# Loading v of the first eight heads in long rows and turning it twice on chip

## The chip, the cores and the metric

The kernel runs on one core of a Trainium2 chip. The metric is device time in microseconds, the median of several runs. A profile of one execution, with every instruction and DMA packet of the core, stands beside it.

## The reference

Two stages follow each other. The first is causal attention for 4 batches, 8 heads, 768 positions and 64 elements per head. Some heads ("retrieval") see all earlier positions, the others only 4 sink positions and a window of 64. The second is a soft mixture of experts over the 3072 resulting rows of 512: 32 slots, 8 experts with 4 slots each, a softmax over the rows to fill the slots and one over the slots to bring the results back.

```python
scores = scale * np.matmul(q, k.transpose(0, 1, 3, 2))
...                                            # causal, sink and window masks per head
a = np.exp(scores - max); a = a / sum          # softmax
x = np.matmul(a, v)                            # -> rows (3072, 512)

logits = x @ phi                               # (3072, 32)
d = softmax(logits, axis=0)
slot_input = (d.T @ x).reshape(8, 4, 512)
for e in range(8):
    slot_out[e] = np.maximum(slot_input[e] @ w1[e], 0) @ w2[e]   # 512 -> 1024 -> 512
out = softmax(logits, axis=1) @ slot_out       # (3072, 512)
```

All inputs lie in HBM in fp32. The kernel loads them with a cast to bf16.

## The kernel before

Attention runs in 16 rounds, one for each pair of heads `n`. Loads are issued from GpSimd into one queue. q and k come in rows of 12 positions, 12 x 64 x 4 = 3072 bytes of HBM, and land with (head, 12 positions) on each partition; TensorE turns them to (64 elements of a head) x (768 positions) by 24 small transposes. v comes with position on the partition, as the product with the probabilities needs it, and so in pieces of 64 elements: 256 bytes in HBM, 128 in SBUF.

```python
def load_qk(pairs, order="qk"):
    t = raw.tile([P, 2, 2, S], BF16, tag="raw", name="raw")       # raw has two buffers
    ...
        nc.gpsimd.dma_start(t[:, z, :len(pairs)],
                            src[b, h:h + c].rearrange("(y h) (p s) d -> (h p) y (s d)", h=2, s=12))

def load_v(m):                                                    # four heads: pairs 2m, 2m + 1
    b, h = m // 2, 4 * (m % 2)
    nc.gpsimd.dma_start(vbs[m % 3].rearrange("p h j d -> p (h j) d")[:, :, :D],
                        v[b, h:h + 4].rearrange("h (j p) d -> p (h j) d", p=P))

def transposes(n, which):
    src = (qraw if which == "q" else kraw)[n]
    tp = trp.tile([P, 12, 64], BF16, tag="tr", name="tp" + which)  # PSUM, trp has two buffers
    for s in range(12):
        for hh in range(2):
            po = slice(64 * hh, 64 * hh + 64)
            nc.tensor.transpose(tp[po, s, :], src[po, 64 * s:64 * s + 64], ident[po, po])
    return tp

def evac(n, which, tp):                                           # PSUM -> SBUF
    dst = qkT.tile([P, S], BF16, tag="T" + which, name="T" + which)
    o, i = dst.rearrange("c (p s) -> c p s", s=12), tp.rearrange("c s p -> c p s")
    if which == "q":
        nc.vector.tensor_copy(o, i)
        qT[n] = dst
    else:
        nc.scalar.copy(o, i)
        kT[n] = dst

def vfar(n):                                                      # v, zeroed for far keys of window heads
    t = vfp.tile([P, 2, 4, 66], BF16, tag="vf", name="vf")
    nc.vector.tensor_mul(t, vb(n)[:, :, :4, :], fmask[:, h:h + 2])
```

A round computes the scores of pair n in six chunks on TensorE, each followed by an exp on ScalarE, and between them the product of the previous pair's probabilities with v (`pvmm`), its division (`norm`), the transposes of the next pair's q and k, and masks on VectorE. The schedule is by hand: each engine works in the order of the program.

```python
load_qk([0], "kq"); load_qk([1]); load_v(0); nc.gpsimd.dma_start(w1s[0], w1v[0])
...
for n in range(NP):                         # 16 pairs
    if n == 0:
        load_qk([2]); load_v(1)
    elif n == 1:
        load_qk([3])
    elif n == 2 or (n % 2 == 1 and n < 12):
        m = 2 if n == 2 else (n + 3) // 2
        load_qk([2 * m, 2 * m + 1]); load_v(m)
    w_load(1 + 5 * (n + 1) // 8)            # next w1, w2: 2 MB of HBM each
    scores(n, 0)
    ...                                     # pvmm(last, 0..2), logits
    scores(n, 1)
    ...                                     # norm(last, 0); transposes and evac of q of pair n + 1; mask(n, 0)
    scores(n, 2)
    ...                                     # pvmm(last, 3); x_transpose(n - 2); mask(n, 1)
    scores(n, 3)
    if 0 < n < NP - 1:
        tk = transposes(n + 1, "k")
    mask(n, 2)
    scores(n, 4)
    if 0 < n < NP - 1:
        evac(n + 1, "k", tk)
    if n >= 1:
        pvmm(last, 4)
    if n:
        vfar(n)
    scores(n, 5)
    if n == 0:
        vfar(0)
    if n >= 1:
        pvmm(last, 5)
        norm(last, 1)
    ...
    if n == 0:                              # pair 1 is turned at the end of round 0
        evac(1, "q", transposes(1, "q")); evac(1, "k", transposes(1, "k"))
    if n < 3:
        far_mask(n + 1)                     # VectorE: masks of the next two heads
        for h in (2 * n + 2, 2 * n + 3):
            head_mask(h)
    elif n == 3:
        setup_late()                        # VectorE: small tiles for the second stage
```

The second stage then fills the slots, multiplies by w1 and w2 and writes the output. The last three w2 go into the buffers of masks and probabilities and can only be loaded when attention is through, in halves of 256 columns: all left halves first, then all right ones. The left half of the first 12 output rows per partition is computed and written before the right halves of w2 are used; `second(e, (1,))` (line 513), `slot_out` (line 560) and the products (line 541) come after them.

Of the kernel before, what the change touches and what calls it, by code (L numbers as in the profile page):

```python
# [11 lines left out]
BF16 = mybir.dt.bfloat16  # L12
# [26 lines left out]
def kernel(  # L39
# [13 lines left out]
    nc = tc.nc  # L53
    P = 128
    B, H, S, D = q.shape
# [14 lines left out]
    xp = ent(tc.tile_pool(name="xp", bufs=2))  # L70
    scp = ent(tc.tile_pool(name="scp", bufs=2, space=PSUM))
    trp = ent(tc.tile_pool(name="trp", bufs=2, space=PSUM))
    pvp = ent(tc.tile_pool(name="pvp", bufs=2, space=PSUM))

    def single(shape, dt, name, tag=None):
        return singles.tile(shape, dt, name=name, tag=tag or name)
# [3 lines left out]
    ident = single([P, P], BF16, "ident")  # L80
# [23 lines left out]
    qraw, kraw, qT, kT, vf, pT, pv, xb = {}, {}, {}, {}, {}, {}, {}, {}  # L104

    def load_qk(pairs, order="qk"):
        b, h, c = pairs[0] // 4, 2 * (pairs[0] % 4), 2 * len(pairs)
        t = raw.tile([P, 2, 2, S], BF16, tag="raw", name="raw")
        for which in order:
            src, d, z = (q, qraw, 0) if which == "q" else (k, kraw, 1)  # L110
            nc.gpsimd.dma_start(t[:, z, :len(pairs)],  # L111
                                src[b, h:h + c].rearrange("(y h) (p s) d -> (h p) y (s d)", h=2, s=12))
            for x, n in enumerate(pairs):
                d[n] = t[:, z, x]

    def load_v(m):
        b, h = m // 2, 4 * (m % 2)
        nc.gpsimd.dma_start(vbs[m % 3].rearrange("p h j d -> p (h j) d")[:, :, :D],  # L118
                            v[b, h:h + 4].rearrange("h (j p) d -> p (h j) d", p=P))

    def vb(n):
        return vbs[n // 2 % 3][:, 2 * (n % 2):2 * (n % 2) + 2]
# [5 lines left out]
    def w_load(upto):  # L128
        while wi[0] < min(upto, 2 * NE - 3):
            e = wi[0] % NE  # L130
            dst, src = ((w1s, w1v), (w2s, w2v))[wi[0] // NE]
            nc.gpsimd.dma_start(dst[e], src[e])
            wi[0] += 1

    def transposes(n, which):
        src = (qraw if which == "q" else kraw)[n]
        tp = trp.tile([P, 12, 64], BF16, tag="tr", name="tp" + which)
        for s in range(12):
            for hh in range(2):
# [4 lines that stand above are left out]
    def evac(n, which, tp):  # L144
# [4 lines that stand above are left out]
            qT[n] = dst  # L149
        else:  # L150
            nc.scalar.copy(o, i)  # L151
            kT[n] = dst

    def vfar(n):
        h = 2 * (n % 4)
        t = vfp.tile([P, 2, 4, 66], BF16, tag="vf", name="vf")
        nc.vector.tensor_mul(t, vb(n)[:, :, :4, :], fmask[:, h:h + 2])
        vf[n] = t

    def scores(n, c):  # L160
        o, ln, parts = CHUNKS[c]
        sc = scp.tile([P, 2, 512], F32, tag="sc", name="sc")
        at = 0
        for j, i0, cnt in parts:
            for hh in range(2):
                po = 64 * hh
                nc.tensor.matmul(sc[:, hh, at:at + 128 * cnt], kT[n][po:po + 64, j * 128:(j + 1) * 128],  # L167
                                 qT[n][po:po + 64, i0 * 128:(i0 + cnt) * 128], start=True, stop=True)
            at += 128 * cnt
        if c == 0:  # L170
            pT[n] = ptp.tile([P, 2, NPT], BF16, tag="pT", name="pT")
        nc.scalar.activation(pT[n][:, :, o:o + ln], sc[:, :, :ln], ACT.Exp, scale=scale)  # L172

    def mask(n, c):
        h = 2 * (n % 4)
        if c == 0:
            x, m = pT[n][:, :, 0:512], msk[:, h:h + 2, 0:512]
        elif c == 1:
            x = pT[n][:, :, 512:1024].rearrange("p h (a c) -> p h a c", a=2)
            m0 = msk[:, h:h + 2, 256:512]  # L180
            m = bass.AP(tensor=m0.tensor, offset=m0.offset, ap=[m0.ap[0], m0.ap[1], [0, 2], [1, 256]])
        else:
            x, m = pT[n][:, :, 1024:1408], msk[:, h:h + 2, 256:640]
        nc.vector.tensor_mul(x, x, m)  # L184

    def pvmm(n, i):
        if i % 3 == 0:
            pv[n] = pvp.tile([P, 3, 2, 65], F32, tag="pv", name="pv")
        for hh in range(2):
            for j in range(i + 1):  # L190
                vv = vb(n) if i - j <= 1 else vf[n]
                o = BLK[j, i]
                nc.tensor.matmul(pv[n][:, i % 3, hh, :], pT[n][:, hh, o:o + 128], vv[:, hh, j, :D + 1],  # L193
                                 start=(j == 0), stop=(j == i))

    def norm(n, half):
        b, h = n // 4, 2 * (n % 4)
        if h == 0 and half == 0:
            xb[b] = xp.tile([P, 6, DM], BF16, tag="xb", name="xb")
        rs = small.tile([P, 3, 2, 1], F32, tag="rs", name="rs")  # L200
        nc.vector.reciprocal(rs, pv[n][:, :, :, 64:65])  # L201
        nc.vector.tensor_mul(  # L202
            xb[b][:, 3 * half:3 * half + 3, h * D:(h + 2) * D].rearrange("p i (h d) -> p i h d", h=2),
            pv[n][:, :, :, :64], rs.to_broadcast([P, 3, 2, 64]))
# [10 lines left out]
    def logits_mm(b, dbs):  # L215
        if b not in lgs:
            lgs[b] = trp.tile([P, 256], F32, tag="tr", name="lg")
        for db in dbs:
            for g in range(3):
                nc.tensor.matmul(lgs[b][32 * g:32 * g + 32, :], phi[:, db], xT[:, db, 256 * g:256 * (g + 1)],  # L220
                                 start=(db == 0), stop=(db == 3))

    def logits_exp(b):
        nc.scalar.activation(expT[:, b], lgs[b][:96], ACT.Exp, accum_out=colpart[:, b:b + 1])  # L224
# [16 lines left out]
    def slot_sum(b):  # L241
        sp = sps[b][0]
        if b == 0:
            nc.vector.tensor_copy(slot_acc, sp)
        else:
            nc.vector.tensor_add(slot_acc, slot_acc, sp)
# [44 lines left out]
    def head_mask(h):  # L291
        V.tensor_scalar(msk[:, h], grade, thr[:, h:h + 1], None, op0=ALU.is_ge)
# [27 lines left out]
    for n in range(NP):  # L320
        if n == 0:
            load_qk([2])
            load_v(1)
# [4 lines that stand above are left out]
            load_qk([2 * m, 2 * m + 1])  # L328
            load_v(m)
        w_load(1 + 5 * (n + 1) // 8)  # L330
        if n == 0:
            nc.gpsimd.dma_start(phi, moe_phi.rearrange("(do di) s -> di do s", di=P))
        b, r = n // 4 - 1, n % 4
        last = n - 1

        scores(n, 0)
        if n >= 1:
            for i in range(3):
                pvmm(last, i)
        if b >= 0 and r == 2:  # L340
            logits_mm(b, (0, 1, 2, 3))

        scores(n, 1)
        if b >= 0 and r == 2:
            logits_exp(b)
        if n >= 1:
            norm(last, 0)
        if 0 < n < NP - 1:
            tq = transposes(n + 1, "q")
            evac(n + 1, "q", tq)  # L350
        mask(n, 0)
        if b >= 0 and r == 3:
            exp_tokens(b)

        scores(n, 2)
        if n >= 1:
            pvmm(last, 3)
        if n >= 2:
            x_transpose(n - 2)
        mask(n, 1)  # L360
# [8 lines that stand above are left out]
            evac(n + 1, "k", tk)  # L369
        if n >= 1:  # L370
            pvmm(last, 4)
        if n:
            vfar(n)

        scores(n, 5)
        if n == 0:
            vfar(0)
        if n >= 1:
            pvmm(last, 5)
            norm(last, 1)  # L380
        if b >= 0 and r == 3:
            dispatch_mm(b)
            slot_sum(b)
        if n == 0:
            evac(1, "q", transposes(1, "q"))
            evac(1, "k", transposes(1, "k"))
        if n < 3:
            far_mask(n + 1)
# [3 lines that stand above are left out]
            setup_late()  # L392
# [212 lines left out]
```

The softmax here doesn't subtract the row's maximum and nothing guards it: scores larger than these inputs give would overflow.

## Time and profile before

| what | value |
|---|---|
| time, median of 3 runs (lowest to highest) | 157.29 us (156.19 to 157.38) |
| span of the profiled execution | 155.7 us |
| busy: TensorE, VectorE, ScalarE | 118.2 (76%), 106.8 (69%), 109.8 (71%) us |
| DMA packets (of these under 512 bytes) | 40535 (26050) |
| v loads: number, size in SBUF, median time from issue to landing | 8, 384 KB, 13.0 us |
| q, k loads of the same size: median time to landing | 6 each, 10.2 and 11.4 us |
| DMA issue on GpSimd: a v load, a q or k load (mean) | 1451 ns, 639 ns |

In the 40 equal slices of the span each digit is the busy share in tenths (9 is 90% or more); PEclk is the granted clock of TensorE, DMA the share of the 16 DMA engines.

```profile
DVE  2896269999987869978769979678735414429700
ACT  3286489979799998999898999999451512408700
PEclk9975559999999999999999999999999999956975
DMA  3999999999999999999999999999999999977995
```

The groups of section 5 give for each line of the kernel, engine and operation the count, the busy time, the mean duration of one, and the idle time before it with what ended it. The three copies that matter for the change are these:

```profile
L148 DVE COPY Tq<-tpq 128x768 bf16<-128x768 bf16 x16 | 15.3, 956 | 4.8 <-PE tpq L141 4.6
L151 ACT COPY Tk<-tpk 128x768 bf16<-128x768 bf16 x16 | 12.9, 805 | 5.0 <-PE tpk L141 5.0
L211 DVE COPY xT<-tpx 128x768 bf16<-128x768 bf16 (+1 forms) x17 | 9.0, 528 | 0.8 <-PE tpx L210 0.8
```

L is the line in the kernel, DVE is VectorE, ACT ScalarE, PE TensorE (PEld its weight loads), POOL GpSimd.

### The profile page before, as it was taken

The page shows a single profiled execution, that of the slowest core. Times are in us where ns is not written, and L with a number is a line of the kernel's source. Part 1 is how long each engine was busy: PE and PEld are TensorE (multiplying, and loading weights), DVE is VectorE, ACT ScalarE, POOL GpSimd, SP SyncE. Part 2 cuts the span into 40 slices and gives each one's busy share as a digit, 9 for nine tenths or more (in the row PEclk, how much of TensorE's full clock was granted, in tenths as well). Part 3 has the DMA queues.
Part 4 walks back from the last instruction along what each step waited for, and adds up shares of the span by engine and source line. Part 5 has one row for each costly group of instructions (what it writes and reads, how often), then busy time and mean ns, then how long its engine had stood idle before and what let it go on. Part 6 is the DMA issues. An engine that isn't in the chain of part 4 may idle for free. (4 is left out here: it accounts for less than half of the span.)

```text
span 155.7 us, 5051 instructions
## 1 busy us (share of the span) xinstructions
PE 118.2 (76%) x2239; PEld 74.6 (48%) x2239; DVE 106.8 (69%) x247; ACT 109.8 (71%) x148; POOL 41.1 (26%) x57
## 2 busy tenths in 40 slices
PE   6756598878697979977979979778987897449500
PEld 2324365555465645755656556555633476214300
DVE  2896269999987869978769979678735414429700
ACT  3286489979799998999898999999451512408700
POOL 7673043720350260170084200000480000700000
PEclk9975559999999999999999999999999999956975
DMA  3999999999999999999999999999999999977995
GB/s 54 155 184 203 172 218 203 196 187 189 212 219 202 188 216 198 186 222 195 186 219 200 185 211 223 213 217 215 210 223 190 199 196 199 240 290 283 404 355 183
DMA packets 40535, 32.85 MB, mean 211 GB/s; under 512 B 26050, under 2 KB 37826, under 8 KB 38594
## 3 DMA queue, kind: packets, MB, share of 16 engines
q0 software_dynamic: 38208, 27.82, 115.1%
q1 hardware_dynamic: 2306, 4.72, 8.1%
q8 instruction: 17, 0.28, 0.7%
q14 instruction: 4, 0.03, 0.1%
HBM read 52.49 MB, written 6.29 MB: 377 GB/s over the span
## 5 line engine op out<-in xcount | busy, mean ns | idle before, releaser
L172 ACT ACTIVATE pT<-sc 128x1024 bf16<-128x1024 f32 (+1 forms) x96 | 83.4, 923 | 9.3 <-PE sc L167 8.8
L167 PE MATMUL sc<-Tq,Tk 64*128 64x256 bf16 (+3 forms) x320 | 36.5, 292 | 13.6 <-ACT Tk L151 10.0
L193 PEld LDWEIGHTS <-pT 128*128 128x128 bf16 x672 | 24.9, 99 | 12.2 <-issue 8.0
L184 DVE TENSOR_TENSOR pT<-pT,msk 128x1024 bf16<-128x1024 bf16 (+1 forms) x48 | 29.3, 639 | 0.2 <-ACT pT L172 0.2
L193 PE MATMUL pv<-vb,pT 128*128 128x65 bf16 x352 | 27.5, 196 | 0.3 <-DVE xb L202 0.3
L193 PE MATMUL pv<-vf,pT 128*128 128x65 bf16 x320 | 25.3, 197 | 0.0
L167 PEld LDWEIGHTS <-Tk 64*128 64x128 bf16 x320 | 11.2, 95 | 22.6 <-ACT Tk L151 13.2
L141 PEld LDWEIGHTS <-raw 64*64 64x64 bf16 x768 | 15.9, 115 | 10.8 <-issue 7.4
L111 POOL DMA_DIRECT2D raw<-in_q_dram x10 | 6.4, 639 | 49.5 <-PE tpk L141 48.3
L148 DVE COPY Tq<-tpq 128x768 bf16<-128x768 bf16 x16 | 15.3, 956 | 4.8 <-PE tpq L141 4.6
L202 DVE TENSOR_TENSOR xb<-pv,rs 128x384 bf16<-128x384 f32 x32 | 17.8, 557 | 1.1
L151 ACT COPY Tk<-tpk 128x768 bf16<-128x768 bf16 x16 | 12.9, 805 | 5.0 <-PE tpk L141 5.0
L201 DVE RECIPROCAL rs<-pv 128x6 f32<-128x6 f32 x32 | 6.2, 193 | 11.9 <-PE pv L193 11.9
L118 POOL DMA_DIRECT2D vb<-in_v_dram x8 | 11.6, 1451 | 1.1 <-issue 0.9
L141 PE MATMUL tpk<-ident,raw 64*64 64x64 bf16 x384 | 9.8, 202 | 2.3 <-DVE Tq L148 1.3
L399 POOL DMA_DIRECT2D w<-in_moe_w_dram x6 | 5.2, 879 | 22.3 <-PE sc L167 20.1
L141 PE MATMUL tpq<-ident,raw 64*64 64x64 bf16 x384 | 9.6, 200 | 1.7 <-DMA raw<-in_q_dram 1.7
L541 PE MATMUL bank<-slot_out,expR 128*128 128x256 bf16 (+1 forms) x36 | 9.2, 368 | 1.9 <-DVE slot_out L556 0.5
L210 PE MATMUL tpx<-ident,xb 128*128 128x128 bf16 x96 | 8.1, 218 | 2.0 <-ACT expT L224 1.1
L211 DVE COPY xT<-tpx 128x768 bf16<-128x768 bf16 (+1 forms) x17 | 9.0, 528 | 0.8 <-PE tpx L210 0.8
L543 ACT ACTIVATE ot<-bank,rrow 128x512 f32<-128x512 f32 x6 | 3.9, 686 | 6.5 <-PE bank L541 6.5
L541 PEld LDWEIGHTS <-expR 128*128 128x128 bf16 x36 | 5.1, 153 | 6.3 <-issue 5.7
(86 smaller groups left out, 117.3 us busy)
## 6 DMA issues: line engine op xcount, KB each, us to landing
w<-in_moe_w_dram POOLq DMA_DIRECT2D x13, 1024.0 KB, 18.3
vb<-in_v_dram POOLq DMA_DIRECT2D x8, 384.0 KB, 13.0
w<-in_moe_w_dram POOLq DMA_DIRECT2D x6, 512.0 KB, 17.8
raw<-in_q_dram POOLq DMA_DIRECT2D x6, 384.0 KB, 10.2
raw<-in_k_dram POOLq DMA_DIRECT2D x6, 384.0 KB, 11.4
out_dram<-ot SPq DMA_DIRECT2D x2, 1024.0 KB, 4.6
out_dram<-oh SPq DMA_DIRECT2D x3, 512.0 KB, 6.3
out_dram<-oh POOLq DMA_DIRECT2D x2, 512.0 KB, 6.8
```

The lines of the kernel that those rows point to most:

```text
L118: nc.gpsimd.dma_start(vbs[m % 3].rearrange("p h j d -> p (h j) d")[:, :, :D], v[b, h:h + 4].rearrange("h (j p) d -> p (h j) d", p=P))
L141: nc.tensor.transpose(tp[po, s, :], src[po, 64 * s:64 * s + 64], ident[po, po])
L148: nc.vector.tensor_copy(o, i)
L151: nc.scalar.copy(o, i)
L167: nc.tensor.matmul(sc[:, hh, at:at + 128 * cnt], kT[n][po:po + 64, j * 128:(j + 1) * 128], qT[n][po:po + 64, i0 * 128:(i0 + cnt) * 128], s ...
L172: nc.scalar.activation(pT[n][:, :, o:o + ln], sc[:, :, :ln], ACT.Exp, scale=scale)
L184: nc.vector.tensor_mul(x, x, m)
L193: nc.tensor.matmul(pv[n][:, i % 3, hh, :], pT[n][:, hh, o:o + 128], vv[:, hh, j, :D + 1], start=(j == 0), stop=(j == i))
L202: nc.vector.tensor_mul(xb[b][:, 3 * half:3 * half + 3, h * D:(h + 2) * D].rearrange("p i (h d) -> p i h d", h=2), pv[n][:, :, :, :64], rs. ...
L210: nc.tensor.transpose(tp[:, i * 128:(i + 1) * 128], xb[b][:, i, hp * 128:(hp + 1) * 128], ident)
L211: nc.vector.tensor_copy(xT[:, hp, i0 * 128:i1 * 128], tp[:, i0 * 128:i1 * 128])
L541: nc.tensor.matmul(op, er[r], slot_out[:, cs], start=True, stop=True)
```

## The change

The first two v loads (the eight heads of batch 0, pairs 0 to 3) take the same form as q and k: rows of 3072 bytes of HBM, landing in a tile of their own. Its buffer is one of the two that later hold the attention output `xb`. What lands is not yet what the product needs, so v is turned twice: 24 small transposes and a ScalarE copy bring it to (head, element) x position, in the same way as k; then six transposes of 128 x 128 and a VectorE copy bring position onto the partitions, into the same `vbs` tile as before. This happens in the rounds 0 to 3, each for its own pair, just before `vfar`. The other six v loads stay as they are. It is meant to spare the queue the small packets at the start, when the rounds wait for data.

```diff
+    vraw = xp.tile([P, 2, 2, S], BF16, tag="xb", name="vraw")
+
     def load_v(m):
         b, h = m // 2, 4 * (m % 2)
+        if m < 2:
+            nc.gpsimd.dma_start(vraw[:, m], v[b, h:h + 4].rearrange("(y h) (p s) d -> (h p) y (s d)", h=2, s=12))
+            return
         nc.gpsimd.dma_start(vbs[m % 3].rearrange("p h j d -> p (h j) d")[:, :, :D],
                             v[b, h:h + 4].rearrange("h (j p) d -> p (h j) d", p=P))
@@
     def transposes(n, which):
-        src = (qraw if which == "q" else kraw)[n]
+        src = vraw[:, n // 2, n % 2] if which == "v" else (qraw if which == "q" else kraw)[n]
@@
             nc.scalar.copy(o, i)
-            kT[n] = dst
+            if which == "k":
+                kT[n] = dst
+            return dst
+
+    def v_blocks(n):
+        vT = evac(n, "v", transposes(n, "v"))
+        tp = trp.tile([P, 6, P], BF16, tag="tr", name="tpv")
+        for j in range(6):
+            nc.tensor.transpose(tp[:, j, :], vT[:, 128 * j:128 * j + 128], ident)
+        nc.vector.tensor_copy(vb(n).rearrange("p h j d -> p j h d")[:, :, :, :D], tp.rearrange("p j (h d) -> p j h d", h=2))
@@
         if n >= 1:
             pvmm(last, 4)
+        if 0 < n < 4:
+            v_blocks(n)
         if n:
             vfar(n)
 
         scores(n, 5)
         if n == 0:
+            v_blocks(0)
             vfar(0)
```

## The prediction

> **What bounds the kernel now.** I read the 40 slices first, then the chain of waits, then the windows cut at the rounds, then the timeline. In the slices the DMA line stands at 9 tenths from slice 2 to slice 37. The chain of waits says what that means for the end:
>
> ```profile
> 115.64 22.18 DMA w<-in_moe_w_dram
> 137.82 0.04 issue
> 137.86 0.64 PE bank L513 x8
> 138.50 0.02 issue
> 138.52 0.44 DVE slot_out L560
> 138.96 0.04 issue
> 139.00 3.97 PE bank L541 x9
> ```
>
> (Start, length, what.) The kernel ends behind the last half of w2, which sits 22.18 us in a full queue. But how far is the compute behind that wait? The timeline of TensorE in the tail:
>
> ```profile
> 131.96 1.62 PE L541 MATMUL bank<-slot_out,expR 128*128 128x256 bf16 x8 [0.25 <-DVE oh L545]
> 133.51 0.40 PE L513 MATMUL bank<-w,hT 128*32 128x256 bf16 x8
> 135.21 0.40 PE L513 MATMUL bank<-w,hT 128*32 128x256 bf16 x8 [1.30 <-DMA w<-in_moe_w_dram]
> 137.86 0.62 PE L513 MATMUL bank<-w,hT 128*32 128x256 bf16 x8 [2.24 <-DMA w<-in_moe_w_dram]
> ```
>
> From the last round to 133.51 nothing in the tail waits for w. After that come three groups of 0.40 us and two waits. Without data waits the three groups end at 133.51 + 1.2 = 134.7 instead of 138.5. So the compute has about 3.8 us of slack; everything that delays the rounds by more than this goes into the time.
>
> The rounds (windows; busy us of PE, PEld, DVE, ACT, POOL, then clock, DMA share, GB/s). They are rounds 1, 2, 3, 4 and 5:
>
> ```profile
> 14.75:23.84 9.09, 7.23 (x111) 4.44 (x112) 4.35 (x10) 5.65 (x7) 3.17 (x5) 0.53 1.55 195
> 23.84:29.85 6.01, 4.97 (x117) 3.45 (x118) 5.91 (x16) 5.77 (x8) 2.57 (x4) 1.00 1.05 203
> 29.85:36.48 6.63, 4.97 (x116) 3.35 (x116) 6.56 (x15) 5.77 (x8) 2.13 (x3) 1.00 1.67 189
> 36.48:43.15 6.67, 4.97 (x116) 3.45 (x117) 6.41 (x25) 5.78 (x8) 1.42 (x2) 1.00 1.60 202
> 43.15:49.00 5.85, 5.05 (x120) 3.46 (x120) 5.26 (x11) 5.81 (x8) 1.98 (x2) 1.00 1.03 213
> ```
>
> Only round 1 has room on all engines. In rounds 2 to 4 VectorE is full (5.91 of 6.01, 6.56 of 6.63, 6.41 of 6.67), because the masks and the late setup are built there. From round 5 on ScalarE is full (5.81 of 5.85). The waits for data in these rounds are two:
>
> ```profile
> 18.33 0.85 PE L141 MATMUL tpq<-ident,raw 64*64 64x64 bf16 x24 [1.66 <-DMA raw<-in_q_dram]
> 33.78 0.57 PE L141 MATMUL tpk<-ident,raw 64*64 64x64 bf16 x24 [0.97 <-DMA raw<-in_k_dram]
> ```
>
> Together 2.6 us; that is all that "rounds that wait for data" have to give.
>
> **What the Trainium skill says.** DMA: Bandwidth & Descriptors, "Why small descriptors are slow (HBM only)": every packet has a fixed cost, so short rows lose bandwidth. The trace agrees. Landing is issue plus time to landing: one k load of 384 KB lands at 42.01 + 13.5 = 55.5 us and the v load behind it at 43.24 + 14.8 = 58.0, so v takes 2.5 us of queue; that k load behind its q (41.31 + 12.3 = 53.6) takes 1.9. PSUM — Partial Sum Buffer, "Engine vs sequencer instructions": the queues of ScalarE and VectorE are strictly first in, first out, so a copy that waits holds up all behind it; in the trace VectorE stands for 1.03 us before 12.59, waiting for v, with the masks of the next heads behind it in its queue. Perfetto Trace Analysis, "Optimization Strategy": the most-contended engine can change over time, and gaps are to be read in their stretch; the windows above show just that.
>
> **The change part by part.**
>
> *Queue.* Two v loads of 3072 packets of 128 bytes become loads with rows like q and k. The second now lands at 8.25 + 13.5 = 21.8, behind k at 7.67 + 11.6 = 19.3: 2.5 us, which become 1.9. The first lands at 3.96 + 8.5 = 12.5, behind k at 3.44 + 5.2 = 8.6: 3.9 us, which become 2 at best. Saved: 0.6 + 1.9 = 2.5 us, and at least 2 x 0.6 = 1.2 if the early straggling has another cause. Queue order is kept, so with a queue that never empties the last w lands 1.2 to 2.5 us sooner, near 136.
>
> *Added work per v block*, four times: 24 small transposes (0.56 us as tpq at full clock, 0.85 at half), a ScalarE copy like Tk (0.80), six 128x128 transposes (0.50, as the x transposes), a VectorE copy like xT (0.55, its source is contiguous; 0.96 if it behaves as Tq). These are a chain: each waits for the one before, and each stands in an in-order queue.
>
> *Round 0.* In the kernel before: transposes of q and k for pair 1 from 12.37, first scores of round 1 at 14.75. Now v lands near 10.6, and its transposes take 12.44 to 13.25. ScalarE is in its exps until 13.39 and copies to 14.2. Six transposes at half clock end at 14.85, the VectorE copy at 15.5. Two PSUM buffers are shared, so q's transposes run 14.85 to 15.65 and k's, needing the buffer of the v copy, 15.65 to 16.35; the Tk copy ends at 17.25. Round 1 starts at 17.3: +2.55.
>
> *Round 1.* q and k of pair 2 are there by 17.6, so the 1.66 us wait is gone. But exp of the sixth chunk follows the v chain: Tk copy to 24.65, v copy to 25.35, six transposes to 25.9, scores of the last chunk, exp at 26.2. Without v blocks it would start at 24.65. So 1.55 us, plus 0.4 because pv and the next scores stand behind it on TensorE. Round 2 starts 2.9 to 3.4 us later than 23.84.
>
> *Rounds 2 and 3.* ScalarE loses 0.8 (copy) + 0.5 (transposes) + 0.3 (scores) + some 0.2 to the following scores = 1.8 us each. VectorE does worse: after its third mask (29.23 in the kernel before) it used to go straight on with vf at 29.15. Now it stands until the second turning is done, 1.7 us, and copies 0.55: 2.2 to 2.5 us each, on an engine without gaps. I take 2.5. In round 3 the wait for k (0.97) goes away, but VectorE's Tq copy ends only 0.4 us before that wait ends now, so only little comes back.
>
> *Sum at the start of round 5:* 3.2 + 2.5 + 2.5 = 8.2 us. After it ScalarE is full, so nothing is caught up: the last round ends near 117 instead of 108.7.
>
> *What the end makes of it.* Compute: slack 3.8, delay 8.2, so slot_out comes 4.4 us later. Queue: the issue of each pair of q, k loads hangs on the k transposes two rounds before. For pairs 8 and 9 it moves from 41.31 to 49.5. The queue before it has work until 31.4 + 20.3 = 51.7 (issue and time to landing of the last w in it), less 2.2 saved = 49.5: it just runs dry, by the time from an issue to its first bytes. That is 1 to 2 us, an estimate: the first k load, issued at 1.27, lands after 3.2 us, and later loads of its size follow each other by 1.4. It happens again in the next three pairs of rounds, about 4 us in all. That gives the saving back; the last w lands near 139, still before compute asks for it at 142. Left output halves are written before the right ones compete, which gives back perhaps 0.7. Result: 157.3 + 4.4 - 0.7 = 161.0 us.
>
> **The rivals.**
>
> *A: the wait for data pays for everything.* Then added work hides in the 2.6 us of waits, the rounds slip by less than 3.8 us, and the full queue alone sets the end: 157.3 - 1.2 to -2.5, some 155.3. For it: DMA is at 9 in nearly all slices and is the longest piece of the chain. Against it: ScalarE alone gets 4 x 0.80 = 3.2 us, more than the waits, and round 0 has no wait that its chain could fill.
>
> *B: ScalarE sets the loss, VectorE does not.* If VectorE catches up (its copy is 0.55 and later rounds leave it slack), each of rounds 2 and 3 costs 1.8 and the missing k wait returns 1.0: 3.2 + 1.8 + 0.8 = 5.8. Less 3.8 leaves 2.0: 159.3, within 2%. For it: ScalarE is the bound from round 5 on. Against it: the row of round 4 (6.67 long, ScalarE 5.78) has VectorE as its limit, so its lag does not vanish.
>
> *C: the half clock lasts.* The clock is at 0.53 in round 1. If the longer stalls of TensorE keep it down through round 2, the transposes of that round take 0.85 instead of 0.56 and it costs 1 to 2 us more: 162 to 163. Nothing in the profile says that it must.
>
> **Range and chances.** My chain gives 161.0; B gives 159.3 and A, which I hold possible but not likely, 155.3. C lies above. The range is 157.0 to 163.5. The limit of 2% is 160.4, just under my number. Slower by over 2%: 0.54. Within: 0.43. Faster by over 2% would need 154.1, below what even A gives: 0.03.
>
> **What would show it.** The two v loads landing some 2 us behind k tells the queue's part. Round 1's first scores near 17.3 and round 2's near 27 check the first steps; the distance from mask to vf on VectorE in rounds 2 and 3, about 2.3 us with the copy, checks the third; round 5 starting near 51 the sum. In the tail the waits of the last w2 groups for DMA should vanish. If these waits remain and the last round ends before 112.4, A or B holds and I am wrong in the stalls: either the chain of a v block overlaps more than I let it, or ScalarE and VectorE have room in rounds that I read as full.

## The result and the profile after

The changed kernel takes 164.64 us (median of 6 runs, 164.07 to 165.18) against 157.33 us (156.19 to 157.59). The ratio is 1.048, with a 95% interval of 1.044 to 1.052. The profiled execution spans 162.2 us instead of 155.7.

The rounds, cut as before at the first scores of rounds 1 to 5 (busy us of PE, PEld, DVE, ACT, POOL, then clock, DMA share, GB/s), in the changed kernel:

```profile
17.36:26.73 9.37, 7.77 (x140) 5.04 (x140) 4.99 (x10) 6.83 (x8) 3.88 (x5) 0.68 1.13 191
26.73:35.05 8.32, 6.62 (x148) 4.50 (x147) 6.02 (x16) 6.46 (x8) 1.40 (x2) 0.88 1.53 176
35.05:43.98 8.93, 7.26 (x149) 5.10 (x147) 6.96 (x15) 6.83 (x9) 2.52 (x3) 0.81 1.43 188
43.98:51.99 8.01, 5.97 (x121) 4.05 (x118) 7.15 (x26) 5.56 (x8) 1.42 (x2) 0.83 0.85 172
51.99:57.93 5.94, 5.15 (x117) 3.40 (x118) 5.42 (x12) 5.69 (x8) 1.97 (x2) 0.95 1.53 176
```

Rounds 2 to 4 (rows two to four) are 2.3, 2.3 and 1.3 us longer than before, and no engine fills them any more: in round 2 VectorE is busy 6.02 us of 8.32, ScalarE 6.46. Added work and standing still are both in there. The timeline of TensorE and VectorE shows the standing still, for the block of round 2 and in round 4:

```profile
31.65 0.56 PE L147 MATMUL tpv<-ident,vraw 64*64 64x64 bf16 x24
33.91 0.51 PE L166 MATMUL tpv<-ident,Tv 128*128 128x128 bf16 x6 [1.70 <-ACT Tv L157]
48.95 0.69 PE L147 MATMUL tpk<-ident,raw 64*64 64x64 bf16 x24 [1.99 <-DVE Tq L154]
```
```profile
31.18 1.15 DVE L199 TENSOR_TENSOR pT<-pT,msk 128x1024 bf16<-128x1024 bf16 x2
34.46 0.56 DVE L167 COPY vb<-tpv 128x768 bf16<-128x768 bf16 x1 [2.12 <-PE tpv L166]
35.05 0.43 DVE L172 TENSOR_TENSOR vf<-vb,fmask 128x528 bf16<-128x528 bf16 x1
```

TensorE turns v at 31.65, then stands 1.70 us for the ScalarE copy; VectorE stands 2.12 us for TensorE, with vf and two divisions behind it. From its third mask to vf (32.33 to 35.05) it takes 2.7 us, in round 3 2.5; the prediction had about 2.3. The wait of TensorE for VectorE in round 4 is now 1.99 us; in the kernel before it was 0.99:

```profile
40.45 0.56 PE L141 MATMUL tpk<-ident,raw 64*64 64x64 bf16 x24 [0.99 <-DVE Tq L148]
```

The last scores of round 15 end at 117.97 instead of 108.90: the rounds slip by 9.1 us.

In the tail the waits for w are gone. TensorE there, and the chain of waits around the right half of slot_out:

```profile
141.02 1.62 PE L559 MATMUL bank<-slot_out,expR 128*128 128x256 bf16 x8 [0.25 <-DVE oh L563]
142.57 0.84 PE L531 MATMUL bank<-w,hT 128*32 128x256 bf16 x24
```
```profile
140.49 1.34 DVE oh L563 x3
141.83 0.04 issue
141.87 0.38 PE bank L559 x2
142.25 0.01 issue
142.26 0.38 PE bank L559 x2
142.64 0.80 PE bank L531 x24
143.44 0.02 issue
143.46 0.43 DVE slot_out L578
```

No DMA is left in the chain. The last w, issued at 124.71, lands 18.2 us later, at 142.9 (137.8 before), and the last groups run through without a wait. slot_out of the right half starts at 143.46, 4.9 us later than before. The queue lost its store of work on the way; in the 40 slices of the changed kernel:

```profile
DMA  3999999999996997999999999999999999979995
GB/s 47 161 218 199 183 221 175 179 176 153 218 212 122 188 207 134 187 196 186 187 199 162 180 198 206 216 224 210 210 226 202 192 199 196 177 237 367 410 360 186
```

Two dips of the DMA digit (the 13th and the 16th, with 122 and 134 GB/s) stand where before there were nines: the loads for pairs 8 to 11 are issued at 49.9 and 62.8, after the queue's last w has nearly landed.

The chain stops at the last instruction of an engine (147.05 before, 151.03 now). The span runs on for 8.7 and 11.2 us with output writes alone, as the windows of the changed kernel show:

```profile
152.00:156.00 4.00, 0.00 (x0) 0.00 (x0) 0.00 (x0) 0.00 (x0) 0.00 (x0) 0.50 0.98 382
156.00:160.00 4.00, 0.00 (x0) 0.00 (x0) 0.00 (x0) 0.00 (x0) 0.00 (x0) 0.50 1.05 347
```

So two things end at nearly the same time, 142.9 and 143.5, and both are 5 us late. Is it the queue that ran dry, or the compute? And does the delay come from the added work or from the way it is chained?

### The profile page after: what moved, and what is told of

The parts are those of the page before. It is cut to its first block, busy times and chain, and to the rows that moved or that the text cites. A ratio compares the mean times of both kernels' runs of the same rounds, so it can differ in the third digit from the quotient of the medians.

```text
span 162.2 us, 5297 instructions
## 1 busy us (share of the span) xinstructions
PE 123.2 (76%) x2357; PEld 79.7 (49%) x2359; DVE 108.1 (67%) x251; ACT 113.2 (70%) x152; POOL 39.4 (24%) x57
## 5 line engine op out<-in xcount | busy, mean ns | idle before, releaser
L182 PE MATMUL sc<-Tq,Tk 64*128 64x256 bf16 (+3 forms) x320 | 38.0, 303 | 11.0 <-ACT Tk L157 7.7
L208 PEld LDWEIGHTS <-pT 128*128 128x128 bf16 x672 | 25.9, 101 | 12.8 <-issue 8.1
L208 PE MATMUL pv<-vb,pT 128*128 128x65 bf16 x352 | 28.5, 200 | 0.3 <-DVE xb L217 0.3
L208 PE MATMUL pv<-vf,pT 128*128 128x65 bf16 x320 | 26.0, 201 | 0.0
L182 PEld LDWEIGHTS <-Tk 64*128 64x128 bf16 x320 | 11.4, 96 | 20.6 <-ACT Tk L157 10.0
L217 DVE TENSOR_TENSOR xb<-pv,rs 128x384 bf16<-128x384 f32 x32 | 17.8, 558 | 1.1
L417 POOL DMA_DIRECT2D w<-in_moe_w_dram x6 | 5.2, 878 | 27.1 <-PE pv L208 25.3
L124 POOL DMA_DIRECT2D vb<-in_v_dram x6 | 8.5, 1422 | 4.3 <-PE pv L208 3.6
L559 PE MATMUL bank<-slot_out,expR 128*128 128x256 bf16 (+1 forms) x35 | 7.7, 304 | 2.4 <-DVE slot_out L574 0.5
L167 DVE COPY vb<-tpv 128x768 bf16<-128x768 bf16 x4 | 2.2, 558 | 10.4 <-PE tpv L166 10.4
L561 ACT ACTIVATE oh<-bank,rrow 128x256 f32<-128x256 f32 x12 | 5.2, 472 | 4.0 <-PE bank L559 3.9
```

The source lines that it names most:

```text
L217: nc.vector.tensor_mul(xb[b][:, 3 * half:3 * half + 3, h * D:(h + 2) * D].rearrange("p i (h d) -> p i h d", h=2), pv[n][:, :, :, :64], rs. ...
L559: nc.tensor.matmul(op, er[r], slot_out[:, cs], start=True, stop=True)
```

## The experiments

Theory S (stalls): a v block is a chain through three in-order engines, each of which stands still; the delayed compute sets the end. Rival Q (queue): the delay matters only because the queue runs dry and the last w comes late. Rival W (work): ScalarE and VectorE are full, and the mere added instructions cost the time. All times are medians beside runs of the kernel before on the same chip.

**e1_no_turn.** The long rows alone. The four blocks are left out, and two tiles hold a constant, so the attention of eight heads is not the reference's.

```diff
+    for t in vbs[:2]:
+        V.memset(t[:, :, :, :D], 0.5)
@@
-        if 0 < n < 4:
-            v_blocks(n)
@@
-            v_blocks(0)
```

> The changed kernel with the long rows of v, but without the eight turnings: the four v blocks are left out and the two v tiles hold a constant from a memset, so the attention of these heads isn't the reference's. It shows the queue's part alone. Both theories (stalls of the chain, queue run dry) expect the rounds to start as in the kernel before or earlier, because the waits for q and k shrink, and the last w to land 1.2 to 2.5 us before 137.8: 154.8 to 156.2 us. A rival, that long rows of v by themselves disturb the early loads, expects 157 or more.

Measured 155.68 us (before 157.31), ratio 0.989 (0.982 to 0.996). The last w, issued at 114.31, lands 21.4 us later, at 135.7, 2.1 us earlier than in the kernel before; the time is 1.6 us shorter. This is what the queue has to give.

**e2_turn_only.** The work alone: short pieces of v as before, the blocks turn a constant and write it where nobody reads.

```diff
+    V.memset(vraw, 0.5)
@@
-        if m < 2:
-            nc.gpsimd.dma_start(vraw[:, m], ...)
-            return
@@
-        nc.vector.tensor_copy(vb(n)..., tp...)
+        nc.vector.tensor_copy(vdump..., tp...)
```

> The v loads of the kernel before (short pieces), with the eight turnings added on a constant tile and their result written to a tile that nobody reads: the work alone. If the loss is all in the work and its stalls, 164 to 166 us, as the changed kernel or a little slower as it lacks the saving in the queue; rounds 2 to 5 start within 0.7 us of the changed kernel's 26.7, 35.1, 44.0, 52.0. If the long rows have a part in the loss, clearly below 164.

Measured 166.31 us, ratio 1.053 (1.045 to 1.061): just above the 164 to 166 expected, and 9.0 us above the kernel before. No part of the loss needs the long rows. Round 0 starts 1.5 us later here (9.42 against 7.91, behind the added memset), so the round starts miss the 0.7 us that I expected; counted from round 0, rounds 2 to 5 start after 18.9, 27.3, 37.0 and 44.4 us, in the changed kernel after 18.8, 27.1, 36.1 and 44.1.

**e3_w_ahead.** Tells Q from the others: one weight load more is in the queue.

```diff
-        w_load(1 + 5 * (n + 1) // 8)
+        w_load((2 if n >= 3 else 1) + 5 * (n + 1) // 8)
```

> The changed kernel with one more weight load issued ahead from round 3 on, so that the queue still has 4.85 us of work when the q and k of the next pairs are issued late; no compute is changed. If the queue that ran dry in rounds 5 to 12 sets the time (last w lands at 142.9 instead of 137.8), the last w lands near 138 and the outputs can start to flow as soon as they are made: 160 to 161.5 us. If the delayed compute alone sets it (slot_out of the right half ready 4.9 us later), at most 1 us is gained: 163.6 to 164.6 us.

Measured 164.14 us, ratio 1.041 (1.033 to 1.048); the interval overlaps that of the changed kernel. The last w, issued at 125.28, lands 15.8 us later, at 141.1: 1.9 us sooner, though not near 138 as I had expected. It does not help. The windows of the tail of e3 (columns as above):

```profile
136.00:140.00 4.00, 3.73 (x65) 2.99 (x69) 0.73 (x2) 0.59 (x1) 0.00 (x0) 0.96 0.99 133
140.00:144.00 4.00, 3.48 (x29) 2.11 (x24) 2.81 (x7) 2.17 (x6) 1.34 (x2) 0.62 0.06 15
144.00:148.00 4.00, 3.15 (x33) 1.92 (x28) 3.03 (x6) 2.58 (x6) 1.60 (x3) 1.00 0.91 303
```

From 140 to 144 the DMA engines do almost nothing (share 0.06) while TensorE is busy 3.48 of 4 us. Q falls as the sole cause: the delayed compute sets the end.

**e4_split.** Tells S from W: the same instructions, but the two turnings of a block lie apart, with other work between.

In round 1 the second chunk of scores also moves ahead of the products with v, which have to wait for the block of pair 0 (diff shortened).

```diff
-    def v_blocks(n):
-        vT = evac(n, "v", transposes(n, "v"))
+    def v_first(n):
+        vTs[n] = evac(n, "v", transposes(n, "v"))
+    def v_second(n):
+        vT = vTs[n]
@@ round 0: after the k transposes of pair 1
+            v_first(0)
@@ round 0: before and after scores(0, 5)
-            v_blocks(0)
-            vfar(0)
@@ round 1: behind scores(1, 0)
+            v_second(0); vfar(0); scores(1, 1)
@@ rounds 1 to 3
         scores(n, 2)
+        if 0 < n < 4:
+            v_first(n)
@@
-            v_blocks(n)
+            v_second(n)
```

> The changed kernel with the two turnings of a v block pulled apart: the first goes between the third and the fourth chunk of scores, the second stays before vf; that of pair 0 goes behind the k transposes of pair 1 and into round 1. Same instructions, same count. If the loss comes from engines that stand still while the chain of one block passes through three of them, the delay of the rounds falls from 9 to 1 to 2.5 us, below the slack of 3.8, the queue never runs dry, and the time is 155 to 157 us. If it is the added work itself (ScalarE 4 x 0.8, VectorE 4 x 0.55 on engines that are full), the rounds still slip by 5 us or more: 160 us or more.

Measured 159.44 us, ratio 1.012 (1.006 to 1.018). The rounds slip by 4.9 us instead of 9.1: neither expectation, though close to that of W. The chaining is nearly half of the delay, so S is shown for that half; 4.9 us remain. Its rounds 2 to 4 cost 1.0, 0.8 and 0.5 us more than before, and then round 5 takes 8.0 us (45.80 to 53.80) where it took 5.7: TensorE ran much of it at the half clock (0.61 on average), 0.85 us for 24 small transposes instead of 0.56, after waiting 1.47 us for VectorE in round 4. The windows of rounds 4 and 5:

```profile
38.66:45.80 7.14, 4.97 (x118) 3.46 (x118) 6.84 (x26) 5.77 (x8) 1.81 (x3) 0.95 1.07 215
45.80:53.80 8.00, 7.32 (x117) 4.63 (x118) 5.31 (x11) 6.10 (x8) 1.57 (x2) 0.61 1.34 195
```

**e5_delay3 and e6_delay9.** A plain delay in the kernel before, five or twelve idle ScalarE copies, to test the slack.

```diff
+    dump = single([P, 768], BF16, "dump")     # the scratch tile
+    V.memset(dump, 0.0)
@@
         scores(n, 0)
+        if n == 4:
+            for _ in range(5):          # 12 in e6
+                nc.scalar.copy(dump, dump)
```

> The kernel before, with five idle ScalarE copies (a scratch tile onto itself) behind the first exp of round 4, and nothing else: a delay of the rounds by some 3 us, with no v block and no change in the loads. If the rounds have 3.8 us of slack behind the full queue, the last w lands at 137.8 as before and the time stays within 0.5 us of 157.3. If the slack isn't there, 159 to 160.5 us.

> The same with twelve copies, a delay of some 8 to 9 us in one place, as large as that of the changed kernel. If the delay of the rounds explains the loss, however it comes about, 163 to 166 us, with the output written later than slot_out by 18.5 instead of 17.2 us. If the v blocks do harm in another way too (clock, long rows), clearly less than the changed kernel, 160 to 162 us.

Measured 160.10 us (ratio 1.019, 1.012 to 1.026) and 165.28 us (1.050, 1.042 to 1.058). The copies delayed the rounds more than I meant, by 4.1 and 10.1 us, and slot_out of the right half came 1.7 and 7.6 us later. So a delay of another origin costs what the v blocks cost (7.9 us of time for 10.1 of delay in e6, 7.3 for 9.1 in the changed kernel). slot_out had 2.4 us of slack here, not 3.8. And in e6 the output did not end 18.5 us behind slot_out, as I had expected, but 17.8; e10 shows why. Where slot_out lost the rest of its slack, the timeline of TensorE in e5 shows:

```profile
133.87 1.47 PE L518 MATMUL bank<-w,hT 128*32 128x256 bf16 x24
135.87 2.91 PE L546 MATMUL bank<-slot_out,expR 128*128 128x256 bf16 x12 [0.53 <-DVE slot_out L561]
138.71 1.47 PE L518 MATMUL bank<-w,hT 128*32 128x256 bf16 x24
```

The 24 matmuls of the last w take 1.47 us, in the changed kernel 0.84: the granted clock was 0.50 there. My slack took the full clock for granted.

**e7_split_late and e8_late_only.** The rest of e4: VectorE is full in round 4 because of a setup of 2.2 us, which nothing needs before the end. It is spread over rounds 5, 6, 8 and 9, in the split kernel and, as a control, in the kernel before.

```diff
-        elif n == 3:
-            setup_late()
+        elif n > 4:
+            setup_late(n)        # its parts for n = 5, 6, 8, 9
```

> The split kernel (159.44 us) with the late setup of VectorE (2.2 us at the end of round 3) taken apart and spread over rounds 5, 6, 8 and 9, where VectorE has room. If a full VectorE and, through the wait it gives TensorE, the half clock of round 5 are what is left of the delay (4.9 us), the rounds slip by 2 to 3 us, below the slack, and the saving in the queue shows: 155 to 156.5 us. If ScalarE's four copies are what is left, 158.5 to 159.5 us.

> The control to it: the kernel before with the late setup spread in the same way. The rounds get 0.5 to 1 us shorter, but the full queue sets the end: within 0.5 us of 157.3 by every theory. If it is faster by more, the gain of the split kernel with this edit isn't the long rows'.

Measured 156.52 us, ratio 0.995 (0.992 to 0.998), and 157.58 us, ratio 1.002 (1.000 to 1.004). In e7 the rounds slip by 1.3 us, less than the 2 to 3 expected, the last w lands at 116.92 + 19.1 = 136.0, and the half clock of round 5 is gone; it beats both kernels, the one before if only by half a per cent. In e8 the rounds end 1.8 us earlier than before and nothing is gained: the queue sets that end. Rounds 1 to 4 of e7:

```profile
15.37:24.34 8.97, 8.06 (x149) 5.48 (x146) 5.62 (x12) 7.01 (x9) 2.74 (x5) 0.68 1.19 215
24.34:31.32 6.98, 5.89 (x146) 4.15 (x147) 6.61 (x16) 6.46 (x9) 2.46 (x4) 1.00 1.48 186
31.32:38.73 7.41, 5.90 (x147) 4.16 (x148) 7.04 (x16) 6.47 (x9) 2.37 (x3) 1.00 1.75 192
38.73:44.43 5.70, 4.90 (x116) 3.35 (x116) 5.26 (x12) 5.66 (x8) 1.91 (x3) 1.00 1.05 216
```

and rounds 2 and 3 of e8:

```profile
23.21:29.27 6.06, 4.97 (x116) 3.45 (x117) 5.96 (x16) 5.77 (x8) 2.57 (x4) 1.00 1.03 205
29.27:35.60 6.33, 5.04 (x117) 3.46 (x118) 6.26 (x15) 5.88 (x8) 2.14 (x3) 1.00 1.70 190
```

In rounds 2 and 3 VectorE is now full again (6.61 of 6.98, 7.04 of 7.41) at full clock, and it waits only 0.27 us for each second turning. Each round is 0.9 to 1.1 us longer than in e8, the like kernel without v blocks: this is what the added work costs there. Over all rounds e7 ends its scores 3.1 us behind e8 (110.17 against 107.12), so W is worth about 3 us at the most; in the 1.3 us it is hidden behind the 1.8 that the spread setup gives in any case. Round 1 is no longer than in the kernel before (8.97 against 9.09), though without a block, in e1, it took 6.86: its wait for data paid for its block.

**e9_after_late.** The fourth corner: the chained blocks, with the setup spread.

> The changed kernel, its v blocks unsplit, with only the late setup of VectorE spread over later rounds. With e4, e7 and the changed kernel this makes a table of two by two. If the two causes (chain of a block, full VectorE in round 4) simply add, the delay of the rounds falls from 9.1 by the 1.8 us that the same edit gave the kernel before: 7 to 7.5 us, and 162 to 163 us. If they feed each other, the delay falls by 3 us or more, and the time is under 162.

Measured 163.29 us, ratio 1.038 (1.032 to 1.044). The rounds slip by 8.0 us. The delays of the four kernels in us:

| | setup in round 3 | setup spread |
|---|---|---|
| blocks chained | 9.1 | 8.0 |
| blocks split | 4.9 | 1.3 |

All four are counted from the kernel before. Without any v block, spreading alone gives -1.8 (e8), so the blocks add 9.1 and 4.9 us in the left column but 9.8 and 3.1 in the right one. The two causes don't simply add: spreading gives 1.1 with the chain and 3.6 without it. The time fits neither expectation, 162 to 163 us or less. In e9 round 4 became 1.7 us shorter (6.34), but round 3 took 9.63 us instead of 8.93. Single traces of the same chained code put round 3 at 8.93, 9.23 (e3) and 9.65 us (e2), so 0.7 us of this is scatter.

**e10_late_left.** The tail. In my prediction the end came 0.7 us closer to slot_out; in the profile it moved 1.5 us away (162.2 - 143.46 = 18.7 against 155.7 - 138.52 = 17.2). The kernel before, with the writes of the left half held back:

```diff
@@ in half_rows, for the left half
-            eng.dma_start(ov[:, r - rows:r, cs], ...)
+            held.append((eng, ov[:, r - rows:r, cs], ...))
@@
     V.tensor_copy(slot_out[:, right], sp[1])
+    nc.gpsimd.tensor_copy(tiny, slot_out[:, 256:264])   # GpSimd waits for slot_out
+    for eng, o, i in held:                              # the four writes of the left half
+        eng.dma_start(o, i)
```

> The kernel before, in which the output of the left half rows is computed at the same time but held back on GpSimd until slot_out of the right half is ready; nothing else is changed. In the profile of before these writes are issued 6 us ahead of that point, in the changed kernel 1.9. If the loss of this lead is what made the end of the changed kernel 1.5 us longer than my prediction had it, the stretch from slot_out to the end grows from 17.2 to 18.7 us or more and the time to 158.5 to 160 us. If not, it stays at 17.2 and 157.3.

Measured 161.42 us, ratio 1.027 (1.019 to 1.034): slower than I expected at the most. slot_out starts at 137.86, 0.7 us earlier than before, but the end is 21.5 us behind it. The windows of the tail of e10:

```profile
132.00:136.00 4.00, 2.25 (x24) 1.34 (x24) 2.19 (x6) 2.28 (x6) 0.00 (x0) 1.00 1.21 162
136.00:140.00 4.00, 2.06 (x12) 0.93 (x13) 1.36 (x3) 0.61 (x1) 1.29 (x3) 0.51 0.06 8
140.00:144.00 4.00, 3.74 (x12) 1.65 (x11) 3.65 (x6) 3.34 (x7) 1.84 (x3) 0.63 0.97 323
```

and of the kernel before:

```profile
132.00:136.00 4.00, 2.22 (x24) 1.31 (x24) 2.00 (x5) 2.08 (x6) 2.94 (x4) 0.99 1.30 228
136.00:140.00 4.00, 1.61 (x11) 0.76 (x11) 0.80 (x2) 0.00 (x0) 0.00 (x0) 0.50 0.85 302
140.00:144.00 4.00, 3.93 (x13) 1.65 (x11) 3.64 (x6) 3.45 (x6) 0.00 (x0) 0.65 0.72 279
```

Before, the left writes stand in the queue behind the last w and fill it at once (302 GB/s from 136 to 140); held back, the DMA engines stand empty (8 GB/s), and all the output has to go out afterwards. The traces of all runs say more than that: where the output does not queue behind w, the end hangs on the first left write and not on slot_out of the right half. This write is issued in the kernel before and in the changed kernel at

```profile
132.51 2.94 POOL L554 DMA_DIRECT2D out_dram<-oh  x4 [15.99 <-ACT oh L543]
```
```profile
141.56 2.95 POOL L572 DMA_DIRECT2D out_dram<-oh  x4 [15.99 <-ACT oh L561]
```

All runs, in us from the span's start:

| run | last w lands | first left write | right slot_out starts | end | write to end | slot_out to end |
|---|---|---|---|---|---|---|
| before | 137.8 | 132.5 | 138.5 | 155.7 | 23.2 | 17.2 |
| e8 | 137.3 | 132.0 | 138.0 | 155.2 | 23.2 | 17.2 |
| e11 | 137.1 | 132.1 | 137.8 | 154.7 | 22.7 | 16.9 |
| e1 | 135.7 | 131.7 | 136.4 | 153.6 | 21.9 | 17.2 |
| e2 | 147.2 | 143.8 | 147.7 | 164.4 | 20.6 | 16.7 |
| e5 | 139.5 | 137.4 | 140.2 | 158.0 | 20.7 | 17.8 |
| e6 | 144.9 | 143.3 | 146.2 | 164.0 | 20.7 | 17.8 |
| e7 | 136.0 | 133.8 | 136.5 | 154.4 | 20.6 | 17.9 |
| e4 | 139.4 | 137.5 | 139.9 | 158.1 | 20.6 | 18.2 |
| e9 | 141.9 | 140.6 | 142.9 | 161.3 | 20.7 | 18.4 |
| e3 | 141.1 | 142.7 | 144.8 | 163.3 | 20.6 | 18.5 |
| changed | 142.9 | 141.6 | 143.5 | 162.2 | 20.6 | 18.7 |
| e10 | 137.2 | 138.9 | 137.9 | 159.3 | 20.4 | 21.5 |

In the last nine rows the end comes 20.4 to 20.7 us after the first left write, whether slot_out of the right half follows it after 3.9 us (e2) or 1.9 (changed kernel). In the first four the write is issued 4.0 us or more before the last w has landed and stands behind it; there the end comes 17.7 to 17.9 us after that landing. e10 moved the four left writes alone, so their effect is shown by an experiment; the constant 20.6 us is read from the traces.

**e11_split_one.** e7 with long rows for the first load only.

```diff
-        if m < 2:
+        if m < 1:
-        if 0 < n < 4:
+        if n == 1:
```

> The split kernel with the late setup spread, with long rows only for the first v load (pairs 0 and 1); the second load is as in the kernel before, and rounds 2 and 3 have no v block. If the first load carries most of the saving (in my working 1.9 of 2.5 us) the last w lands 1.3 to 2 us before 137.8, the rounds are not later than in the kernel before, and the time is 155.3 to 156.5, not above the 156.52 of the kernel with both. If both loads save the same 0.6 us, 156.6 to 157.3.

Measured 156.55 us, ratio 0.994 (0.992 to 0.997), the same as e7. But the last w lands at 114.85 + 22.2 = 137.1, only 0.7 us earlier than before, so the first load does not carry most of the saving; the time was right for another reason. This kernel issues the first left write 1.7 us sooner than e7 but has it behind w, which lands 1.1 us later; the two ends come out 0.4 us apart. With short pieces the first load landed between 11.1 (e6) and 12.8 us (e2) in different kernels: the 3.9 us that I had read from one trace were in part chance.

## Why the prediction was wrong

It said 161.0 us, within 157.0 to 163.5; measured were 164.64. The direction and the stalls were right. What failed is the step "What the end makes of it", and the sum of the rounds was somewhat small.

*Queue.* Saved 1.2 to 2.5 us: e1 shows 2.1, and the two v loads land 2.0 and 1.8 us behind k. That it would run dry was right in kind and too small in size: I had the last w near 139, it landed at 142.9. This did not cost the miss, as e3 shows.

*Round by round.* Round 1 at 17.3: measured 17.36. Round 2 at 3.2 us late: 2.9. Rounds 2 and 3 at 2.5 each: 2.3 each. Then the sum stops at the start of round 5 with 8.2 us, because I let round 4 keep its length; it grew by 1.3 us, with TensorE's wait for VectorE 1.0 us longer and the granted clock at 0.83. With the late setup moved out of it (e9) it was 1.7 us shorter. At the start of round 5 the delay was 8.8 us, at the end of the rounds 9.1: 0.9 more than I carried on. Rival C, the half clock, was therefore partly true. Rival B, in which VectorE catches up and the blocks cost 5.8 us, does not hold as it stands. Most of the 9.1 us is the way the blocks are chained and their clash with the late setup: with the same instructions it comes down to 1.3 us (e7), of which spreading the setup would give -1.8 in any case (e8), so some 3 us at the most are the work itself.

*The end.* "Compute: slack 3.8, delay 8.2, so slot_out comes 4.4 us later", and left halves "written before the right ones compete, which gives back perhaps 0.7": together a credit of 4.5 us against the delay. slot_out did come 4.9 us later for 9.1 of delay, so its slack was 4.1, though at the half clock it is 2.4 (e5, e6). But it is not what the end hangs on. The chain of waits of the kernel before stops at the last instruction and leaves out the writes behind it, and I took the path up to there for the path to the end. The left half of slot_out never waited for the last w, so the first left write slipped by the whole 9.1 us (132.51 to 141.56). In the kernel before it stood behind w, with 23.2 us to the end; without that it is 20.6. This cover of 2.6 us was the real slack: 9.1 - 2.6 = 6.5 us, which is the difference of the spans (162.2 - 155.7). I had 3.7: of the 2.8 between, 1.9 are the credit of 4.5 that was only 2.6, and 0.9 the rounds. The same 2.5 to 2.6 us fit e2 to e6 and e9.

The two profiled executions took 157.49 and 164.31 us, 6.8 apart; the rest to the 7.3 of the medians is scatter of single executions. One reading was loose: the nines of the DMA line end with slice 35 and not 37, and the two sevens behind them lie where the first output is written.

## What to carry to other kernels

Put a chain through several in-order engines into a schedule with other work between its links; one after the other, each engine stands for the links on the others (in round 2 here TensorE 1.7 us and VectorE 2.1, for copies of 0.8 and transposes of 0.5). A wait that stands last on the path is slack for what runs beside it, but not the same slack for each: work that does not wait there, as the left half of the output here, has less of it. Follow the path to the last output write and not to the last instruction. What a shorter transfer can give is measured quickest by leaving the work around it out (e1): here 1.6 us, while the chained work alone cost 9.0 (e2).

## What the runs showed of the hardware

Waits of TensorE can cost it the clock: in e5 and e6, which only add ScalarE copies to the kernel before, it stood 4.0 and 10.05 us in round 4, and the granted clock of that round was 0.75 and 0.64 instead of 1.00. With shorter waits the two go together, but no run varies the wait alone. In the changed kernel, with waits of 1.6 to 2.0 us in rounds 1 to 4, the clock of rounds 2 to 4 was 0.88, 0.81 and 0.83 instead of 1.00; in e4 one wait of 1.47 us in round 4 was followed by a round 5 at 0.61 that took 2.3 us longer. Not each such wait did it: after the one of 1.60 us that ended at 42.84 in the changed kernel the clock stayed at 1.00 until 49.2, and waits of about 1 us in the kernel before left it at 1.00.

Pieces of 128 bytes are not very dear when the queue is deep: 2.5 us for 384 KB against 1.9 in rows of 1.5 KB. That would make 1.2 us for two loads; e1 had the last w 2.1 us earlier, and the rest stays unexplained. The output of 6.3 MB took 20.6 to 20.7 us from the issue of its first write in the eight runs in which that write neither stood long behind w nor was held back.
